# The first units and the first weights of a fused attention and two-MLP kernel in another order

## The chip, the cores and the metric

The kernel runs on one core of a Trainium2 chip. The metric is the time of one execution on the device in microseconds. Three runs of the kernel before took 1079.28, 1087.26 and 1090.63 us; their median, 1087.26 us, is the time before. The engines are TensorE (PE in the rows; PEld is its weight load), VectorE (DVE), ScalarE (ACT), GpSimd (POOL) and SyncE (SP). ACTq and SPq are the instruction queues of ScalarE and SyncE, which also issue DMAs.

## The reference

Decay attention over q, k, v of shape (4, 8, 576, 64), then two MLPs on 2304 tokens of 512 features. In short:

```
log_f  = log(clip(f, 0.0001, 1.0));  cum = cumsum(log_f, axis=-1)
scores = q @ k.T / sqrt(64) + cum[..., :, None] - cum[..., None, :]   # causal
attn   = softmax(scores);  x = attn @ v          # x: (2304, 512)
h = x @ w1_in;  x = (h * sigmoid(1.702 * h)) @ w1_out    # 512 -> 2048 -> 512
h = x @ w2_in;  out = (max(h,0) + alpha * min(h,0)) @ w2_out
```

The MLP weights come as float64 and everything is computed to nearly float32 precision: an operand is split into a rounded high part and a low part (KH, KL and so on), and a product is the sum of three.

## The kernel before

**The plan.** The kernel does not issue its work directly. Each piece is added to a list with a cost per engine that could do it, the buffers it reads and writes, and a priority (`Plan.add`). `Plan.run` then simulates the list: at each step it takes, among all pieces whose inputs are there, the one that can start first, and only between equal start times the one with the lower priority number. A DMA on SP or on ScalarE (`ACTQ`) holds its queue for 480 ns in this plan and ends 1150 ns plus transfer plus 750 ns later. A piece that several engines may do goes to the one that would end it first, with a bias. The order found is the order of the program on each engine; on the chip every engine follows it strictly, so an instruction that waits holds all those behind it. Buffers of a pool (SBUF tiles, PSUM banks) are handed out in the order in which the code created them.

**The start.** f is loaded (L365), clipped (L421) and its logarithm taken (L422). Then the running sums of log f are made in two parts, positions 0 to 255 and 256 to 575 (L427 on): transposes on TensorE (`lf_tr`, L434), copies (`lf_cp`, L439), products with a triangle (`cum_mm`, L448), evacuation by ScalarE (L457), rounding and subtraction on VectorE (L458, L459), and two DMAs to a DRAM scratch (L462, L463). Both parts have priorities near -80, ahead of all units.

**Units.** Attention is cut into 32 units: first positions 0 to 255 of all 16 pairs of heads, then the rest. `prep` loads k and q of a unit in four DMAs each (L510, tiles rk and rq), transposes them (L514), splits them, and loads the sums into DK: the first four units straight from SBUF (L530), the others from the scratch (L535). It loads v (L544, tile VR). The k and q loads of the first 16 units may go to SP or to ScalarE. `chunk` makes the scores once (L598), masks them and finds row maxima (L607, tile MX), and turns these into DQ (L623, L632, L634). `chunk2` makes the scores again with the maxima taken off (L659), the exponential (L663), the product with v (L679) and the division (L718 to L738); the result goes to xr. k and q have two raw buffers each and one buffer for the transposed form.

**The first MLP.** Its first 8 of 16 slices of weights (wA) are loaded and converted from float64 while the first units run (`weight`, `convert`: a DMA at L471 into one of three raw buffers, then L475 to L483 and a split, on ScalarE, VectorE and GpSimd, through two work buffers wc). When the four units of a batch are done, `mlp1a` runs their 256 tokens through these 8 slices: L751 and L793 are its products, L757 and L758 the activation. The tokens and partial sums go to DRAM; the other 8 slices and the second MLP follow on blocks of 512 tokens (L875, L904).

Priorities: unit i is prepared at 100 + i - 2 and computed at 100 + i, slice m of the weights at 105 + 0.6 m, `mlp1a` at 1000 and more.

Of the kernel before, what the change touches and what calls it, by code (L numbers as in the profile page):

```python
# [7 lines left out]
F32 = mybir.dt.float32  # L8
F32R = mybir.dt.float32r
I32 = mybir.dt.int32  # L10
U32 = mybir.dt.uint32
AF = mybir.ActivationFunctionType
# [58 lines left out]
class Plan:  # L71
# [32 lines left out]
    def run(self):  # L104
        free = {}
        dma = 0.0
        avail = [o for o in self.ops if o.nd == 0]
        out = []
        while avail:
            best = None  # L110
            for o in avail:
                t0 = o.ready
                need = {}
                for b in o.bufs:
                    t0 = max(t0, b.begin)
                    if b.pool is not None and b.slot is None:
                        p = b.pool
                        r = p.ready()
                        i = need[p] = need.get(p, -1) + 1
                        if p.nxt + i != b.idx or len(p.free) <= i or p.nxt + i - p.gone >= p.n or r is None:  # L120
                            t0 = None
                            break
                        t0 = max(t0, r, p.free[i][0])
                if t0 is None:
                    continue
                alt = None
                for eng, dur, *more in o.alts:
                    bias, port = (*more, 0.0, False)[:2] if len(more) < 2 else more
                    t = max(t0, free.get(QUEUE.get(eng, eng), 0.0))
                    if port:  # L130
                        t = max(t, free.get("port", 0.0))
                    if eng in QUEUE:
                        end = max(t + 1150.0, dma) + dur + 750.0
                    else:
                        end = t + dur
                    key = end + bias
                    if alt is None or key < alt[0]:
                        alt = (key, t, eng, end, port)
                _, t, eng, end, port = alt
                if best is None or (t, o.pri, end, o.seq) < best[0]:  # L140
                    best = ((t, o.pri, end, o.seq), o, eng, port)
# [4 lines left out]
            if eng in QUEUE:  # L146
                free[QUEUE[eng]] = t + 480.0
                dma = end - 750.0
# [9 lines left out]
            for b in o.bufs:  # L158
                b.left -= 1
                b.end = max(b.end, end + LAT)  # L160
                if b.left == 0 and b.pool is not None:
                    p = b.pool
# [19 lines left out]
def kernel(  # L182
# [13 lines left out]
    nc = tc.nc  # L196
# [4 lines left out]
    P = 128  # L201
    BH = B * H
    NP = H // 2
    KT = DM // P
# [4 lines left out]
    EARLY = 4  # L209
    ACTQ = 16  # L210
    PRE = 2
# [3 lines left out]
    BLK = 256  # L215
    SPLIT = 256

    plan = Plan()
    E = {"PE": nc.tensor, "DVE": nc.vector, "ACT": nc.scalar, "POOL": nc.gpsimd, "SP": nc.sync, "ACTQ": nc.scalar}


    const = ctx.enter_context(tc.tile_pool(name="const", bufs=1))
# [20 lines left out]
    def sb(reg, nm, slots, shape, dt=F32, after=()):  # L243
        p = Pool(slots, after)

        def make(i):
            side, cl = closing[reg]
            return open_region(reg, side, cl).tile(shape, dt, name=f"{nm}{i}", tag=f"{nm}{i}")

        p.make = make  # L250
        return p
# [5 lines left out]

    wA = sb("res", "wA", NA, [P, 2, 2 * KT, P], F32R)
    p_raw8 = sb("res", "wraw", 3, [P, 4, P, 2], I32)
    p_wc = sb("res", "wc", 2, [P, 4, P])  # L260
    p_xh = sb("m1a", "xh", 3, [P, 2, BLK], F32R)
    p_xl = sb("m1a", "xl", 2, [P, 2, BLK], F32R)
    p_g = {n: sb("m1a", n, 2, [P, BLK], d) for n, d in (("gg", F32), ("gh", F32R), ("gl", F32R))}
# [60 lines left out]
    ident = const.tile([P, P], F32, name="ident")  # L324
    ident_r = const.tile([P, P], F32R, name="ident_r")
    alpha_sb = const.tile([P, NM], F32, name="alpha_sb")
    order = tc.manual_schedule()
    order.__enter__()

# [35 lines left out]
    plan.add(DMA(BH * S * 4), lambda e: nc.sync.dma_start(f_sb(), f.rearrange("b h s -> (b h) s")), (), [b_f], -100)  # L365

    def set_ident(e):
        nc.gpsimd.memset(ident, 0.0)
        nc.gpsimd.affine_select(ident, ident, pattern=[[-1, P]], compare_op=ALU.not_equal, fill=1.0, base=0, channel_multiplier=1)

# [50 lines left out]
    plan.add([("DVE", 370.0)], lambda e: nc.vector.tensor_scalar(f_sb(), f_sb(), 1e-4, 1.0, op0=ALU.max, op1=ALU.min), (), [b_f], -80)  # L421
    plan.add([("ACT", 600.0)], lambda e: nc.scalar.activation(f_sb(), f_sb(), AF.Ln), (), [b_f], -80)  # L422

    b_ch = Buf()
    chi = lambda: xr[0:BH, 3, RING - S:].bitcast(F32R)
    b_lt = Buf(ps_h)
    for part, (lo, hi) in enumerate(((0, SPLIT), (SPLIT, S))):  # L427
        ts_ = [t for t in range(NKT) if lo <= t * P < hi]
        pri = -80 + part

        def lf_tr(e, ts_=ts_):
            for t in ts_:
# [30 lines left out]
        plan.add(DMA(128 * (hi - lo)), lambda e, cs=cs: nc.sync.dma_start(cscr[1, :, cs], cuml()[:, cs].bitcast(F32)), [(b_cc, part)], [(b_cum, (part, 1))], pri + 0.5)  # L463
    plan.add(DMA(8192), lambda e: nc.sync.dma_start(alpha_sb, alpha.rearrange("(m p) -> p m", p=P)), (), [b_alpha], 300)

    def convert(wb, half, src, pri):

        raw, w = Buf(p_raw8), Buf(p_wc)
        sl = slice(half * KT, (half + 1) * KT)
        n = KT * P  # L470
        plan.add(DMA(P * n * 8), lambda e: nc.sync.dma_start(raw.ap.rearrange("p c n t -> p c (n t)"), src), (), [raw], pri)  # L471
        low, high = lambda: raw.ap[:, :, :, 0], lambda: raw.ap[:, :, :, 1]
        wi = lambda: w.ap.bitcast(I32)

# [9 lines left out]
        plan.add(a_copy(n), lambda e: copy(e, wb.ap[:, 0, sl], w.ap), [w], [(wb, (half, 0))], pri)  # L484
        plan.add(a_sub(n), lambda e: sub(e, wb.ap[:, 1, sl], w.ap, wb.ap[:, 0, sl].bitcast(F32)), [w, (wb, (half, 0))], [(wb, (half, 1))], pri)

    def weight(pool, w_in, w_out, m, pri):
        wb = Buf(pool)
        convert(wb, 0, w_in[:, m * P:(m + 1) * P].bitcast(I32).rearrange("(c p) n -> p c n", p=P), pri)
        convert(wb, 1, w_out[m * P:(m + 1) * P, :].bitcast(I32).rearrange("p (c n) -> p c n", c=KT), pri + 0.1)  # L490
        return wb

    W1, W2 = {}, {}
# [318 lines left out]

    b_xs, b_yp, b_y1 = Buf(), Buf(), Buf()
    done = {"c": 0}
    A0, A1 = 100.0, 10.0

    def advance(t, pri):
        while done["c"] < NT // BLK and (done["c"] + 1) * BLK <= t:
# [4 lines left out]
    seq = [(b, hp, q0, q1) for q0, q1 in ((0, SPLIT), (SPLIT, S)) for b in range(B) for hp in range(NP)]  # L823
    pend = []
    for i, (b, hp, q0, q1) in enumerate(seq):
        unit = prep(b, hp, q0, q1, A0 + i - PRE, i < EARLY, i < ACTQ)
        pend.append((chunk(unit, q0, q1, A0 + i), col0(b, q0) + q1 - q0 if hp == NP - 1 else 0))
        if i == NP:
            for m in range(NA):
                W1[m] = weight(wA, w1_in, w1_out, m, A0 + 5 + m * 0.6)  # L830
        if len(pend) > 1:
            x, t = pend.pop(0)
            chunk2(x)
            advance(t, 0)
# [124 lines left out]
```

## Time and profile before

| | |
|---|---|
| median of three runs | 1087.26 us (1079.28 to 1090.63) |
| profiled execution | 1090.33 us, span 1088.6 us |
| TensorE busy | 1040.8 us (96% of the span), 6531 matmuls |
| VectorE busy | 696.0 us (64%) |
| ScalarE busy | 448.3 us (41%) |
| GpSimd busy | 124.8 us (11%) |
| mean granted TensorE clock | 0.98 of full speed |

The span goes from the first to the last instruction; the profiled execution's own time is 1.7 us longer than it. The page's row of forty slices of the span (27 us each) shows TensorE at 4, 8, 6 and 7 tenths in the first four and at 9 or more until the last, and its granted clock below full speed in the first five. Matmuls overlap each other and their ends are modelled, so a busy TensorE is not one at its peak.

### The profile page before, as it was taken

What the parts mean: (1) busy time and instruction counts of PE and PEld (TensorE: products, weight loads), DVE (VectorE), ACT (ScalarE), POOL (GpSimd) and SP (SyncE); (2) the same over time, 40 slices, a digit from 0 to 9 for tenths busy, and PEclk for the clock granted to TensorE, in tenths of its full rate; (3) what the DMA queues carried; (4) which work ended last, traced back from release to release, by engine and by line L of the source; (5) the groups of instructions that cost most, each with busy time, mean ns of one, the idle gap of its engine ahead of it and who ended that gap; (6) DMA issues with size and microseconds to landing.
All of it is one profiled execution on the core that took longest, in us unless ns stands there. A gap on an engine that the chain in (4) does not pass through costs nothing.

```text
span 1088.6 us, 17737 instructions
## 1 busy us (share of the span) xinstructions
PE 1040.8 (96%) x6531; PEld 885.5 (81%) x6531; DVE 696.0 (64%) x1560; ACT 448.3 (41%) x1041; POOL 124.8 (11%) x196
## 2 busy tenths in 40 slices
PE   4867999999999999999999999999999999999997
PEld 2656888898999988998888888788888888888885
DVE  5878887788879875969963459743534333544433
ACT  3656655665555554857742347310201211211101
POOL 5321221221221211000100001200000000000000
PEclk8887899999999999999999999999999999999999
DMA  4666564242332110755742325400100200100001
GB/s 76 136 170 156 126 152 97 44 94 47 63 74 60 42 33 10 246 153 176 230 135 97 107 87 177 134 1 1 68 1 1 67 1 1 39 21 20 1 1 39
DMA packets 170055, 86.54 MB, mean 79 GB/s; under 512 B 127440, under 2 KB 155280, under 8 KB 169968
## 3 DMA queue, kind: packets, MB, share of 16 engines
q1 hardware_dynamic: 159360, 84.13, 28.7%
q10 hardware_dynamic: 10608, 1.28, 0.8%
q8 instruction: 51, 0.84, 0.3%
q14 instruction: 36, 0.29, 0.1%
HBM read 66.34 MB, written 19.02 MB: 78 GB/s over the span
## 4 chain that ended last, share of the span: by engine, by line
PE 69%; DVE 4%; ACT 1%; issue 1%; DMA 1%; SPq 0%; ACTq 0%
PE bk L751 30%; PE bk L904 18%; PE bk L875 8%; PE bk L793 5%; PE bk L659 3%; PE bk L708 2%; PE bk L598 1%; PE bk L685 1%; DVE wraw L480 0%; DVE wB L357 0%; PE bk L679 0%; DMA wraw<-in_moe_w_in_dram 0%; DVE wc L483 0%; DVE qgg L762 0%; DVE qgl L357 0%
## 5 line engine op out<-in xcount | busy, mean ns | idle before, releaser
L352 ACT CAST qgh<-qgg 128x512 fp32r<-128x512 f32 (+1 forms) x120 | 69.2, 577 | 337.6 <-DVE qgg L765 314.7
L762 DVE TENSOR_SCALAR qgg<-bk,alpha_sb 128x512 f32<-128x512 f32 (+1 forms) x80 | 55.5, 695 | 166.8 <-PE bk L751 166.8
L751 PE MATMUL bk<-qx,wB 128*128 128x512 f32 (+1 forms) x720 | 156.9, 370 | 0.0
L751 PEld LDWEIGHTS bk<-qx,wB 128*128 128x128 f32 x720 | 125.9, 188 | 24.5
L751 PE MATMUL bk<-xh,wA 128*128 128x256 f32 x576 | 122.6, 293 | 2.6 <-DVE wA L357 1.5
L357 DVE TENSOR_TENSOR qgl<-qgg,qgh 128x512 fp32r<-128x512 f32 (+1 forms) x116 | 75.4, 650 | 67.6 <-ACT qgh L352 59.0
L751 PE MATMUL bk<-qx,wA 128*128 128x512 f32 (+1 forms) x480 | 104.2, 369 | 0.0
L751 PEld LDWEIGHTS bk<-xh,wA 128*128 128x128 f32 x576 | 95.7, 192 | 10.4 <-issue 3.8
L751 PEld LDWEIGHTS bk<-qx,wA 128*128 128x128 f32 x480 | 83.9, 188 | 16.4
L793 PE MATMUL bk<-gh,wA 128*128 128x256 f32 x576 | 85.3, 292 | 6.4 <-ACT DQ L632 2.4
L607 DVE CUSTOM_DVE_ANT_0 bk<-bk,mask 128x512 f32<-128x512 f32 (+3 forms) x160 | 75.0, 493 | 15.5 <-PE bk L598 12.0
L793 PEld LDWEIGHTS bk<-gh,wA 128*128 128x128 f32 x576 | 76.2, 196 | 9.6 <-ACT DQ L632 2.5
L751 PE MATMUL bk<-xl,wA 128*128 128x256 f32 x288 | 81.9, 284 | 1.1 <-DVE xl L357 1.1
L663 ACT ACTIVATE e<-bk 128x320 f32<-128x320 f32 (+3 forms) x224 | 65.2, 365 | 29.9 <-PE bk L659 28.2
L904 PE MATMUL bk<-wA,qgh 128*128 128x512 f32 x288 | 74.1, 396 | 0.5 <-ACT qgh L352 0.5
L904 PEld LDWEIGHTS bk<-wA,qgh 128*128 128x128 f32 x288 | 53.6, 188 | 14.0 <-ACT qgh L352 1.2
L357 POOL TENSOR_TENSOR qx<-qxb,qx 128x512 fp32r<-128x512 f32 (+1 forms) x12 | 15.0, 1257 | 432.9 <-ACT qx L352 387.7
L751 PEld LDWEIGHTS bk<-xl,wA 128*128 128x128 f32 x288 | 55.4, 192 | 1.3 <-DVE xl L357 1.3
L667 POOL TENSOR_SCALAR_AFFINE_SELECT e<-e 128x256 f32<-128x256 f32 (+1 forms) x80 | 32.7, 421 | 199.4 <-ACT e L663 175.8
L475 ACT ACTIVATE wc<-wraw 128x512 f32<-128x512 f32 x64 | 43.2, 678 | 28.8 <-DVE wA L357 9.4
L904 PE MATMUL bk<-wB,qgh 128*128 128x512 f32 x216 | 54.4, 391 | 0.0
L875 PE MATMUL bk<-qgh,wB 128*128 128x512 f32 (+1 forms) x240 | 54.3, 368 | 0.0
(149 smaller groups left out, 2052.9 us busy)
## 6 DMA issues: line engine op xcount, KB each, us to landing
wraw<-in_moe_w_in_dram SPq DMA_DIRECT2D x32, 512.0 KB
wraw<-in_moe_w_out_dram SPq DMA_DIRECT2D x32, 512.0 KB
xscr<-xr SPq DMA_DIRECT2D x9, 512.0 KB
rk<-in_k_dram SPq DMA_DIRECT2D x64, 72.0 KB
ypscr<-yp SPq DMA_DIRECT2D x18, 256.0 KB
VR<-in_v_dram SPq DMA_DIRECT2D x32, 128.0 KB
qxb<-xscr SPq DMA_DIRECT2D x16, 256.0 KB
qyp<-ypscr SPq DMA_DIRECT2D x16, 256.0 KB
```

Source lines behind the costliest of these rows:

```text
L352: nc.scalar.copy(dst, src)
L357: E[e].tensor_tensor(dst, a, b, op=ALU.subtract)
L475: plan.add([("ACT", c_act(n))], lambda e: nc.scalar.mul(w.ap, high().bitcast(F32), 2.0 ** -112), [raw], [w], pri)
L607: plan.add([("DVE", c_dve(c1 - c0) + 90.0)], lambda e, pm=pm, c0=c0, c1=c1, mk=mk, m0=m0, col=col: nc.vector.tensor_tensor_reduce(pm.ap[:, ...
L659: nc.tensor.matmul(pss[hh].ap[:w, :m], x.ap[r, a:a + w], y.ap[r, s0 - q0:n], start=i == 0, stop=i == 3)
L663: plan.add([("ACT", c_act(m, True))], lambda e, hh=hh, pss=pss, e32=e32, w=w, m=m: nc.scalar.activation(e32.ap[:w, hh, :m], pss[hh].ap[:w, ...
L667: plan.add([("POOL", 150.0 + 0.82 * 2 * w, 0.0, True)], lambda e, e32=e32, w=w: nc.gpsimd.affine_select(e32.ap[:w, :, :w], e32.ap[:w, :, : ...
L751: nc.tensor.matmul(ph.ap[:, :n], wb.ap[:, a, c, :], x(c), start=(c == 0 and i == 0), stop=(c == KT - 1 and i == 2))
L762: plan.add([("DVE", c_dve(n) + 56)], lambda e: nc.vector.tensor_scalar(g.ap[:, :n], ph.ap[:, :n], 0.0, alpha_sb[:, m:m + 1], op0=ALU.min, ...
L793: nc.tensor.matmul(py[d // 2].ap[:, d % 2 * BLK:(d % 2 + 1) * BLK], W1[m].ap[:, a, KT + d, :], g.ap, start=(m == 0 and i == 0 and a == 0 a ...
L875: nc.tensor.matmul(py[d].ap[:, :n], W1[m].ap[:, a, KT + d, :], g.ap[:, :n], start=(m == NA and i_ == 0 and a == 0), stop=(m == NM - 1 and ...
L904: nc.tensor.matmul(py[t].ap, g.ap[:, t * P:(t + 1) * P], wo[:, a, KT * P:], start=(m == 0 and i_ == 0 and a == 0), stop=(m == NM - 1 and i ...
```

## The change

The assumed latency of a DMA in the plan rises from 1150 to 1500 ns. The first two units' k and q loads may go to SP only. A one-element exponential (`warm`) is put behind the logarithm. The second part of the sums gets priority 104.5 in place of -79. The first 8 slices of weights get 104 + 0.6 m in place of 105 + 0.6 m, and the loads of the slices 0 and 1 get 101 and 102. There is a third work buffer wc.

```diff
@@ -130,7 +130,7 @@
                     if eng in QUEUE:
-                        end = max(t + 1150.0, dma) + dur + 750.0
+                        end = max(t + 1500.0, dma) + dur + 750.0
@@ -215,6 +215,7 @@
+    A0 = 100.0
@@ -257,7 +258,7 @@
-    p_wc = sb("res", "wc", 2, [P, 4, P])
+    p_wc = sb("res", "wc", 3, [P, 4, P])
@@ -324,6 +325,7 @@
+    warm = const.tile([1, 1], F32, name="warm")
@@ -365,6 +367,7 @@
     def set_ident(e):
+        nc.gpsimd.memset(warm, 0.0)
@@ -421,12 +424,13 @@
+    plan.add([("ACT", 1300.0)], lambda e: nc.scalar.activation(warm, warm, AF.Exp), [b_f, b_id], (), -79)
...
-        pri = -80 + part
+        pri = -80 if part == 0 else A0 + 4.5
@@ -463,12 +467,12 @@
-    def convert(wb, half, src, pri):
+    def convert(wb, half, src, pri, lpri=None):
...
-        plan.add(DMA(P * n * 8), lambda e: nc.sync.dma_start(raw.ap.rearrange("p c n t -> p c (n t)"), src), (), [raw], pri)
+        plan.add(DMA(P * n * 8), lambda e: nc.sync.dma_start(raw.ap.rearrange("p c n t -> p c (n t)"), src), (), [raw], pri if lpri is None else lpri)
@@ -484,10 +488,10 @@
-    def weight(pool, w_in, w_out, m, pri):
+    def weight(pool, w_in, w_out, m, pri, lpri=None):
@@ -823,11 +826,11 @@
-        unit = prep(b, hp, q0, q1, A0 + i - PRE, i < EARLY, i < ACTQ)
+        unit = prep(b, hp, q0, q1, A0 + i - PRE, i < EARLY, 2 <= i < ACTQ)
...
-                W1[m] = weight(wA, w1_in, w1_out, m, A0 + 5 + m * 0.6)
+                W1[m] = weight(wA, w1_in, w1_out, m, A0 + 4 + m * 0.6, A0 + 1 + m if m < 2 else None)
```

## Rows read from the trace of the kernel before

**Rows 1.** Stages: length, each engine's busy us (instructions), granted clock, DMA share, GB/s.

```profile
0.00:20.00 20.00, 6.01 (x27) 3.03 (x27) 9.23 (x30) 6.14 (x11) 13.32 (x40) 1.00 0.43 77
20.00:30.50 10.50, 8.16 (x50) 6.43 (x52) 6.06 (x24) 3.10 (x8) 2.18 (x4) 0.52 0.57 113
64.00:72.00 8.00, 5.18 (x28) 4.62 (x30) 6.21 (x18) 5.63 (x15) 1.09 (x2) 0.57 0.60 151
81.00:92.00 11.00, 8.57 (x52) 6.66 (x50) 6.95 (x18) 7.15 (x18) 0.81 (x2) 0.54 0.46 123
0.00:128.00 128.00, 91.29 (x681) 72.39 (x681) 96.39 (x307) 70.63 (x177) 39.44 (x79) 0.84 0.57 135
128.00:1088.60 960.60, 949.50 (x5852) 813.12 (x5851) 599.59 (x1254) 377.70 (x866) 85.41 (x117) 1.00 0.26 72
```

**Rows 2.** Same view (order PE, PEld, DVE, ACT, POOL), 27 to 108 us.

```profile
27.00:108.00 81.00, 61.18 (x482) 49.35 (x481) 66.41 (x212) 47.57 (x122) 19.53 (x29) 0.84 0.62 154
```

**Rows 3.** ScalarE in time order: start, duration, instruction, [idle before, releaser].

```profile
0.81 0.91 ACTq L510 DMA_DIRECT2D rk<-in_k_dram  x2
1.76 1.28 ACT L352 ACT_TABLE_LOAD   x1 [1.76 <-PEq L943]
3.05 0.30 ACT L352 CAST ident_r<-ident 128x128 fp32r<-128x128 f32 x1
5.29 1.97 ACTq L510 DMA_DIRECT2D rq<-in_q_dram  x2
7.29 1.28 ACT L422 ACT_TABLE_LOAD   x1 [3.94 <-DMA rq<-in_q_dram]
8.59 0.68 ACT L422 ACTIVATE xr<-xr 32x576 f32<-32x576 f32 x1
```

**Rows 4.** VectorE in time order, from the clip to the first mask.

```profile
2.97 0.92 DVE L421 TENSOR_SCALAR xr<-xr 32x576 f32<-32x576 f32 x1 [2.97 <-DMA xr<-in_f_dram]
...
16.24 0.32 DVE L458 CAST xr<-xr 32x320 fp32r<-32x320 f32 x1 [0.95 <-ACT xr L457]
...
16.99 0.48 DVE L459 TENSOR_TENSOR xr<-xr 32x320 fp32r<-32x320 f32 x1
...
17.87 0.27 DVE L607 CUSTOM_DVE_ANT_0 bk<-bk,mask 128x128 f32<-128x128 f32 x1
```

**Rows 5.** TensorE in time order, 0 to 17 us.

```profile
9.41 0.65 PE L434 MATMUL bk<-ident,xr 32*128 32x32 f32 x5 [9.41 <-ACT xr L422]
10.44 4.49 PE L448 MATMUL bk<-xr 128*32 128x256 f32 x14 [0.38 <-DVE xr L439]
...
16.43 0.33 PE L598 MATMUL bk<-DK,ones 64*128 64x128 f32 x2 [1.25 <-DMA DK<-xr]
```

**Rows 6.** SP's DMA issues in time order, first 15 us.

```profile
0.81 0.40 SPq L365 DMA_DIRECT2D xr<-in_f_dram  x1
...
4.21 1.45 SPq L510 DMA_DIRECT2D rk<-in_k_dram  x3
...
13.14 0.32 SPq L462 DMA_DIRECT2D cscr<-xr  x1
...
14.03 1.25 SPq L530 DMA_DIRECT2D DK<-xr  x2
```

**Rows 7.** ScalarE in time order, around the first exponential.

```profile
23.90 1.28 ACT L663 ACT_TABLE_LOAD   x1 [1.80 <-DMA rq<-in_q_dram]
25.20 0.38 ACT L663 ACTIVATE e<-bk 128x256 f32<-128x256 f32 x1
```

**Rows 8.** SP, ScalarE and TensorE in time order, lines that concern early weights.

```profile
27.06 0.45 SPq L471 DMA_DIRECT2D wraw<-in_moe_w_in_dram  x1
...
61.77 0.66 ACT L475 ACTIVATE wc<-wraw 128x512 f32<-128x512 f32 x1 [2.04 <-DMA wraw<-in_moe_w_in_dram]
...
66.82 0.91 PE L659 MATMUL bk<-DQ,DK 64*128 64x256 f32 x2 [3.77 <-ACT DQ L632]
```

**Rows 9.** Waits of TensorE, 0 to 128 us: us in total, times, longest.

```profile
PE bk L751 <- DVE wA L357: 1.5, 2, 1.1
```

More of the change, by code (lines that the diff above doesn't have):

```diff
@@ L485, in convert @@
         plan.add(a_sub(n), lambda e: sub(e, wb.ap[:, 1, sl], w.ap, wb.ap[:, 0, sl].bitcast(F32)), [w, (wb, (half, 0))], [(wb, (half, 1))], pri)
-    def weight(pool, w_in, w_out, m, pri):
+    def weight(pool, w_in, w_out, m, pri, lpri=None):
         wb = Buf(pool)
-        convert(wb, 0, w_in[:, m * P:(m + 1) * P].bitcast(I32).rearrange("(c p) n -> p c n", p=P), pri)
-        convert(wb, 1, w_out[m * P:(m + 1) * P, :].bitcast(I32).rearrange("p (c n) -> p c n", c=KT), pri + 0.1)
+        convert(wb, 0, w_in[:, m * P:(m + 1) * P].bitcast(I32).rearrange("(c p) n -> p c n", p=P), pri, lpri)
+        convert(wb, 1, w_out[m * P:(m + 1) * P, :].bitcast(I32).rearrange("p (c n) -> p c n", c=KT), pri + 0.1, lpri)
         return wb
@@ L814 @@
     done = {"c": 0}
-    A0, A1 = 100.0, 10.0
     def advance(t, pri):
```

## The prediction

> **What bounds the kernel now.** I read the stage table first, then the time order of single engines at the start. TensorE bounds the run. After 128 us it is busy 949.5 of 960.6 us at the full clock; before 128 us only 91.3 of 128, at a mean granted clock of 0.84 [rows 1]. So what a new order can give lies in the first 128 us: 36.7 us of idle time, and about 91.3 x 0.16 = 14.6 us lost because part of the work runs at 1.2 GHz. Single stretches show that second loss: 20 to 30.5, 64 to 72 and 81 to 92 us have granted clocks of 0.52 to 0.57, each after a gap on TensorE [rows 1]. From 27 to 108 us VectorE is busy 66.4 of 81 us: nearly a bound of its own, as all conversions and masks go through it [rows 2]. I assume that work moved earlier on TensorE in this first part shortens the end one for one, since nothing after 128 us waits.
>
> The order at the start is set by ScalarE. It loads a table until 3.04 us and casts until 3.35, then issues two loads of q from 5.29 to 7.26, and only then loads the table for the logarithm, which runs from 8.59 to 9.27 [rows 3]. The input of that logarithm was ready at 2.97 + 0.92 = 3.89 us [rows 4]. TensorE waits for it from the start, 9.41 us [rows 5]; SP stands until 13.14 us for the first half of the sums [rows 6]; the first product with DK comes at 16.43 us [rows 5].
>
> **The change part by part.** The profiled execution took 1090.33 us (span 1088.6); the median of the three runs is 3.07 us lower, 1087.26. The sum is made against 1090.33 and carried over to the median.
>
> *Loads of units 0 and 1 leave ScalarE.* Without the two q issues the logarithm's table load can follow the cast: 3.35 + 1.28 = 4.63, after the 3.89 of its input, so the logarithm starts near 4.65 instead of 8.59, 3.9 us earlier. The chain behind it (transposes, products, evacuation, rounding, DMA into DK) took 16.43 - 9.27 = 7.2 us, so the first product with DK moves to 12.5. Cover needed: units 0 and 1 then have 16 loads of q and k and 4 of v on SP, 20 in all. Three of SP's take 1.45 us, 0.48 each [rows 6]; after f, at 1.21 us, that is 20 x 0.48 = 9.6 us, ending at 10.8, and DK's two issues (1.25 us) can go by 12.1 if all 20 stand ahead of them. The sums reach SP 3.9 us earlier than 13.14, at 9.2; with the planner's priorities the write of the sums goes ahead of the last loads. So SP hides it, with little room. Price: -3.9; bounds 0 (SP is late by as much) and -5.
>
> *Units 2 to 15 may still be put on ScalarE.* Unit 2's loads become free once the first transposes are done, near 5 us, and SP then has a backlog, so they go to ScalarE, in front of the evacuation of the sums (L457). Bounds: 0, and +2.0 (a pair of issues lasted 1.97) [rows 3]. I take +0.9, the other pair of that row group (0.91), since the long one is not explained by anything the trace shows.
>
> *Early table for the exponential.* The load of 1.28 us at 23.90 stands right in front of the first exponential at 25.20 [rows 7], whose result unit 0 waits for. It moves behind the logarithm (4.65 + 0.68 = 5.3 to 6.6 us), plus one activation of one element and one memset of one element on POOL, which I cost at nothing: ScalarE's next work there, the cast of unit 0's k, took place at 9.18 before, and its q comes later still. Cover gone: 1.28 us on the first cast. Price -1.3; bounds 0 (the scores are late for another reason) and -1.3. The Trainium skill (ScalarE: Activation LUTs, What ACT_TABLE_LOAD costs) puts a switch at about 2.66 us, the load and a drain; the exponential 0.02 us after the load's end shows no drain here, and by the page the sum would be 1.4 us lower. The same page (Table sets: the hidden batching unit) says that logarithm and exponential share a set, by which nothing would be saved; the row with a load of its own for the exponential speaks against it in this kernel.
>
> *Late half of the sums.* Its rounding and subtraction on VectorE (0.32 and 0.48 us) stand ahead of unit 0's first mask at 17.87 [rows 4], though its inputs were there earlier: -0.8 on the path. They, three small copies and TensorE's products (about 3.0 of the 4.49 us of that row [rows 5]) have to run somewhere. The planner takes the operation that can start first and uses the priority only between equals, and the bank pool hands out buffers in order of creation, so unit 0's output bank can't be taken before the late half's bank has been. So the half moves only some microseconds, into gaps of TensorE. Bounds -0.8 and +3.0 (its products in front of unit 0's scores, not preempted). I take -0.8: gaps of over 3 us are there. Its two DMAs to DRAM are read only by the units from 16 on.
>
> *Weights.* The first weight load is issued at 27.06 us [rows 8]; the conversions get a priority one unit earlier, the loads of m = 0 and 1 four and three units earlier, and there is a third work buffer. Conversion time is the same in sum. TensorE waited 1.5 us in total for the halves that VectorE writes (L751) [rows 9]. Price -1.5; bounds 0 and -6.5 (the second rival below). One unit's preparation is pushed back by as much VectorE work as is pulled forward; it is ahead of TensorE by then.
>
> *Assumed latency 1500 for 1150.* It changes the order of DMAs everywhere, costs no instruction, and after 128 us TensorE has its work ready: 0; bounds -2 and +2 (a fifth of the 11.1 us of idle time there [rows 1]).
>
> Sum: -3.9 + 0.9 - 1.3 - 0.8 - 1.5 = -6.6, so 1083.7 for an execution like the profiled one, and 1080.7 from the median.
>
> **The rivals.** *More than the sum.* At 61.77 us ScalarE stands 2.04 us for a weight transfer, with the row maxima of a unit queued behind it, and TensorE stands 3.77 us until 66.82 and then runs at the low clock [rows 8]. If early weights remove that wait, the stretch 64 to 72 gives back its idle 2.8 us and 5.18 x 0.43 = 2.2 us of clock, 5.0 in all; the stretch 81 to 92 is worth 2.4 + 8.57 x 0.46 = 6.4 in the same way. One or both besides the sum: 1069 to 1076. For it: the cause is a weight that came late. Against: only two of eight are pulled forward, and the load at 61.77 is of a later one.
>
> *Given back.* VectorE's 82% from 27 to 108 us [rows 2] is the limit, and units that start earlier wait for it later; or the transfers set the pace, not the engine that issues them. The latter is the view of the Trainium skill (DMA: Bandwidth & Descriptors, Issuing engines are not separate DMA queues): issuing from several engines saves only issue time, usually little beside the transfer. Against that as a mechanism here: ScalarE's 3.9 us wait ends with its own issue, not with a landing [rows 3]. A quarter to a half of the sum stays: 1084 to 1086.
>
> *Slower, by SP.* If a load on SP costs what the long pair did on ScalarE (0.98 each), 20 loads end at 1.21 + 19.7 = 20.9 us and DK's issue comes 6.9 us later than its 14.03 [rows 6]. Against this stand -1.3 and -0.8: +4.8, and 1092; if the longer gap costs another low stretch, 1097. It decides from (14.03 - 1.21) / 20 = 0.64 us per load, where SP has shown 0.48, and only if the planner leaves all loads in front.
>
> *It doesn't do what it says.* Priorities being ties only, the late half stays ahead of the first masks and the weights come no sooner: -4.3, 1083.
>
> **How the numbers follow.** Forecast 1081 (1077 to 1084): 0.42. More: 0.25. Given back: 0.21. Slower: 0.07. No effect of the priorities: 0.05. The three runs of before lie 11 us apart, so 1% (10.9 us) is about what a measurement can tell. Faster by over 1% is under 1076.4: nearly all of the second case and the lower edge of the first, 0.33. Slower by over 1% (over 1098): the far end of the SP case and the noise, 0.04. The rest 0.63. The range 1068 to 1091 leaves out the rest of the SP case and the lowest of the second.
>
> **What would show it.** The logarithm before 5.5 us, the first product with DK near 12.5 to 13.5, no table load after 10 us, the first exponential about 5 us earlier than 25.20, TensorE's idle time to 128 us near 31 instead of 36.7 us. The prediction is wrong if SP issues DK after 14 us, if the products of the late half stand right in front of unit 0's scores, or if the low-clock stretches after 60 us number more or fewer than before: each weighs as much as the whole forecast.

## The result, and the profile after

The changed kernel takes 1077.09 us (median of 8 runs, 1075.21 to 1078.60) where the kernel before took 1086.49 us beside it (8 runs, 1079.28 to 1090.63): ratio 0.991, 95% interval 0.9891 to 0.993, or 9.4 us less. The forecast was 1081 us from 1087.26, a gain of 6.6; so the time lies in the range, 4 us under the forecast. The profiled execution took 1075.87 us with a span of 1074.1, and is 14.5 us shorter in span than the profiled one of before, which at 1090.33 us was one of the slowest of its kernel. Lines after the new ones are shifted by 2 to 4: L457 is now L461, L598 is L602, L607 is L611, L663 is L667, L751 is L755, L875 is L878 and L904 is L907.

The stages first, with the columns of [rows 1] (length, then busy us of TensorE, weight load, VectorE, ScalarE, GpSimd, granted clock, DMA share, GB/s):

```profile
0.00:20.00 20.00, 9.23 (x48) 5.80 (x49) 9.98 (x35) 8.19 (x16) 13.48 (x41) 0.81 0.51 99
20.00:30.50 10.50, 10.19 (x64) 7.20 (x64) 8.73 (x34) 7.64 (x19) 4.55 (x7) 0.50 0.67 154
64.00:72.00 8.00, 7.39 (x46) 6.18 (x47) 7.55 (x22) 4.89 (x13) 1.92 (x3) 0.61 0.53 144
81.00:92.00 11.00, 10.04 (x88) 8.54 (x88) 10.82 (x32) 8.98 (x25) 4.99 (x6) 1.00 0.60 154
0.00:128.00 128.00, 99.85 (x781) 79.97 (x782) 102.48 (x327) 77.83 (x196) 45.34 (x86) 0.85 0.61 142
128.00:1074.00 946.00, 933.92 (x5752) 806.33 (x5751) 587.84 (x1238) 370.04 (x847) 80.13 (x106) 1.00 0.26 72
```

TensorE is idle for 128 - 99.85 = 28.1 us before 128 us, 36.7 before, and has issued 781 products there instead of 681. Behind that it still has 12 us of idle time.

ScalarE's start answers to [rows 3] and [rows 7] (start, duration, instruction, [idle before, releaser]):

```profile
3.71 0.68 ACT L425 ACTIVATE xr<-xr 32x576 f32<-32x576 f32 x1
4.41 1.28 ACT L427 ACT_TABLE_LOAD   x1
5.70 0.20 ACT L427 ACTIVATE warm<-warm 1x1 f32<-1x1 f32 x1
...
10.32 1.91 ACTq L514 DMA_DIRECT2D rq<-in_q_dram  x4
12.35 1.85 ACTq L514 DMA_DIRECT2D rk<-in_k_dram  x2
14.24 0.43 ACT L461 ACTIVATE xr<-bk 32x320 f32<-32x320 f32 x1 [5.79 <-DMA rq<-in_q_dram]
...
19.98 0.83 ACT L667 ACTIVATE e<-bk 128x256 f32<-128x256 f32 x3
```

The logarithm starts at 3.71 instead of 8.59 us, the first exponential at 19.98 instead of 25.20, with no table load in front of it. But ScalarE is idle for 5.79 us before the late half's evacuation (14.24). Up to 10.17 us the products that it reads are still running (the row at 5.57 below, 4.60 us long); for the other 4 us it stands behind six loads, issued from 10.32 to 14.20, that the planner put on ScalarE for later units. VectorE passes that on; the same view of VectorE, for [rows 4]:

```profile
14.71 0.51 DVE L462 CAST xr<-xr 32x320 fp32r<-32x320 f32 x1 [3.04 <-ACT xr L461]
15.14 0.40 DVE L359 TENSOR_TENSOR KL<-tk,KH 128x256 fp32r<-128x256 f32 x1
15.47 0.28 DVE L611 CUSTOM_DVE_ANT_0 bk<-bk,mask 128x128 f32<-128x128 f32 x1
```

The first mask starts at 15.47, though its scores were done at 13.0: it is behind the late half's rounding on its engine. TensorE and SP for [rows 5], [rows 6] and [rows 8]:

```profile
5.57 4.60 PE L452 MATMUL bk<-xr 128*32 128x256 f32 x14 [0.38 <-DVE xr L443]
...
12.11 0.35 PE L602 MATMUL bk<-DK,ones 64*128 64x128 f32 x2 [1.69 <-DMA DK<-xr]
12.24 0.53 PE L602 MATMUL bk<-KH,QH 64*128 64x256 f32 x2
12.51 0.48 PE L602 MATMUL bk<-DK,ones 64*128 64x256 f32 x2
17.17 0.42 PE L627 MATMUL bk<-ident_r,MX 128*99 128x128 f32 x1 [4.17 <-DVE MX L611]
...
64.61 0.96 PE L663 MATMUL bk<-DQ,DK 64*128 64x256 f32 x2 [6.40 <-DVE DQ L638]
```

```profile
9.22 0.67 SPq L534 DMA_DIRECT2D DK<-xr  x1
...
14.51 0.40 SPq L475 DMA_DIRECT2D wraw<-in_moe_w_in_dram  x1
```

All 14 products of the sums still run in one block (4.60 us), so the late half was not deferred on TensorE. The first weight load is issued at 14.51 instead of 27.06. The stall of 3.77 us near 66 us [rows 8] did not go: it is 6.40 us now, and ends with VectorE's part of DQ instead of ScalarE's.

**Where the 14.5 us between the spans are.** In every kernel of this study the same 3,771 products stand ahead of the first one of line L875 (L878 after), so that product, between 480 and 490 us, is a clean milestone:

```profile
486.70 1.98 PE L875 MATMUL bk<-qgh,wB 128*128 128x512 f32 x8
```

```profile
480.32 1.98 PE L878 MATMUL bk<-qgh,wB 128*128 128x512 f32 x8
```

(Before first, then after.) 6.4 us are gained up to there, though single profiles of one order differ by as much as 4.4 us in it (E1 below). The rest, 1088.6 - 486.7 = 601.9 us, has become 1074.1 - 480.3 = 593.8 us: 8.1 us come from a stretch that no edit of the order aims at, and in which TensorE hardly waits. There the profile shows this, in time order from the kernel before and then from the changed one:

```profile
726.79 4.36 PE L751 MATMUL bk<-qx,wB 128*128 128x512 f32 x18
730.99 1.98 PE L904 MATMUL bk<-wB,qgh 128*128 128x512 f32 x8
...
999.66 0.63 PE L904 MATMUL bk<-wA,qgh 128*128 128x512 f32 x2
1000.13 1.10 PE L904 MATMUL bk<-wA,qgl 128*128 128x512 f32 x4
1001.07 2.03 PE L904 MATMUL bk<-wA,qgh 128*128 128x512 f32 x8
1002.93 1.10 PE L904 MATMUL bk<-wA,qgl 128*128 128x512 f32 x4
```

```profile
723.46 4.24 PE L755 MATMUL bk<-qx,wB 128*128 128x512 f32 x18
727.54 1.98 PE L907 MATMUL bk<-wB,qgh 128*128 128x512 f32 x8
...
999.76 1.98 PE L907 MATMUL bk<-wA,qgh 128*128 128x512 f32 x8
1001.58 1.07 PE L907 MATMUL bk<-wA,qgl 128*128 128x512 f32 x4
```

The same eighteen products start over 730.99 - 726.79 = 4.20 us before and over 727.54 - 723.46 = 4.08 us after: 233 and 227 ns each, at the full clock, with no wait. Eight products of wA and qgh go from 1002.93 - 1001.07 = 1.86 to 1001.58 - 999.76 = 1.82 us. The engine's busy time can't show it, as it is 100% in both.

What differs is the placement. The 4-byte tile `warm` takes 32 bytes on the left side of SBUF, and every left-hand tile behind it (wA, wC, wraw, the second qx) moves by 32 bytes modulo 64; the right-hand ones (wB, the first qx, qgh, qgl) stay. In the addresses that the built programs give their tiles, the first wA starts at byte 33984 before (0 modulo 64) and the first qgh at 219104 (32 modulo 64); after, that wA is at 34016, 32 modulo 64 as well. Products whose stationary and moving operand differ by 32 modulo 64 run at the slower pace.

### The profile page after: what moved, and what is told of

Read it like the earlier page. It is cut to its first block, busy times and chain, and to the rows that moved or that the text cites. A ratio compares the mean times of both kernels' runs of the same rounds, so it can differ in the third digit from the quotient of the medians.

```text
span 1074.1 us, 17787 instructions
## 1 busy us (share of the span) xinstructions
PE 1033.8 (96%) x6531; PEld 886.3 (83%) x6531; DVE 690.3 (64%) x1565; ACT 447.9 (42%) x1042; POOL 125.5 (12%) x192
## 4 chain that ended last, share of the span: by engine, by line
PE 51%; DVE 3%; DMA 2%; ACT 1%; issue 0%; SPq 0%; DVEq 0%; ACTq 0%
PE bk L755 26%; PE bk L907 18%; PE bk L878 6%; DMA wraw<-in_moe_w_out_dram 1%; PE bk L797 1%; DVE wraw L484 1%; DVE wA L359 1%; DVE wc L487 0%; DVE qgg L762 0%; ACT wraw L480 0%; DVE qgl L359 0%; ACT wc L479 0%; DMA qxb<-xscr 0%; DVE wc L481 0%; DMA out_dram<-qyp 0%
## 5 line engine op out<-in xcount | busy, mean ns | idle before, releaser
L755 PE MATMUL bk<-qx,wB 128*128 128x512 f32 (+1 forms) x720 | 155.8, 368 | 0.0
L755 PEld LDWEIGHTS bk<-qx,wB 128*128 128x128 f32 x720 | 125.9, 189 | 22.7
L755 PE MATMUL bk<-xh,wA 128*128 128x256 f32 x576 | 120.6, 292 | 0.0
L755 PE MATMUL bk<-qx,wA 128*128 128x512 f32 (+1 forms) x480 | 103.6, 368 | 0.0
L755 PEld LDWEIGHTS bk<-xh,wA 128*128 128x128 f32 x576 | 95.3, 192 | 7.0 <-issue 4.0
L755 PEld LDWEIGHTS bk<-qx,wA 128*128 128x128 f32 x480 | 84.2, 188 | 15.3
L797 PE MATMUL bk<-gh,wA 128*128 128x256 f32 x576 | 82.9, 287 | 3.9 <-ACT gh L354 3.2
L755 PE MATMUL bk<-xl,wA 128*128 128x256 f32 x288 | 81.9, 284 | 1.1 <-DVE xl L359 1.1
L611 DVE CUSTOM_DVE_ANT_0 bk<-bk,mask 128x512 f32<-128x512 f32 (+3 forms) x160 | 75.2, 492 | 10.1 <-PE bk L602 8.3
L797 PEld LDWEIGHTS bk<-gh,wA 128*128 128x128 f32 x576 | 73.8, 191 | 7.6 <-ACT gh L354 3.9
L667 ACT ACTIVATE e<-bk 128x320 f32<-128x320 f32 (+3 forms) x224 | 66.5, 364 | 22.4 <-PE bk L663 21.4
L907 PE MATMUL bk<-wA,qgh 128*128 128x512 f32 x288 | 71.9, 389 | 0.0
L907 PEld LDWEIGHTS bk<-wA,qgh 128*128 128x128 f32 x288 | 53.8, 188 | 11.0
L671 POOL TENSOR_SCALAR_AFFINE_SELECT e<-e 128x256 f32<-128x256 f32 (+1 forms) x80 | 33.6, 432 | 208.4 <-ACT e L667 180.6
L755 PEld LDWEIGHTS bk<-xl,wA 128*128 128x128 f32 x288 | 55.4, 192 | 1.4 <-DVE xl L359 1.3
L878 PE MATMUL bk<-qgh,wB 128*128 128x512 f32 (+1 forms) x240 | 54.3, 368 | 0.8 <-ACT qgh L354 0.8
L907 PE MATMUL bk<-wB,qgh 128*128 128x512 f32 x216 | 53.9, 390 | 0.0
L755 PE MATMUL bk<-qx,wC 128*128 128x512 f32 (+1 forms) x240 | 52.8, 368 | 0.0
```

What stands on the lines that cost most here:

```text
L611: plan.add([("DVE", c_dve(c1 - c0) + 90.0)], lambda e, pm=pm, c0=c0, c1=c1, mk=mk, m0=m0, col=col: nc.vector.tensor_tensor_reduce(pm.ap[:, ...
L667: plan.add([("ACT", c_act(m, True))], lambda e, hh=hh, pss=pss, e32=e32, w=w, m=m: nc.scalar.activation(e32.ap[:w, hh, :m], pss[hh].ap[:w, ...
L671: plan.add([("POOL", 150.0 + 0.82 * 2 * w, 0.0, True)], lambda e, e32=e32, w=w: nc.gpsimd.affine_select(e32.ap[:w, :, :w], e32.ap[:w, :, : ...
L755: nc.tensor.matmul(ph.ap[:, :n], wb.ap[:, a, c, :], x(c), start=(c == 0 and i == 0), stop=(c == KT - 1 and i == 2))
L797: nc.tensor.matmul(py[d // 2].ap[:, d % 2 * BLK:(d % 2 + 1) * BLK], W1[m].ap[:, a, KT + d, :], g.ap, start=(m == 0 and i == 0 and a == 0 a ...
L878: nc.tensor.matmul(py[d].ap[:, :n], W1[m].ap[:, a, KT + d, :], g.ap[:, :n], start=(m == NA and i_ == 0 and a == 0), stop=(m == NM - 1 and ...
```

## The experiments

Placement and order were separated first. All ratios are to the kernel before, run beside the experiment on the same chip; where an experiment is set against the changed kernel or against another one, the difference is that of the two ratios, times 1087 us. (A ratio is worked out from all runs and need not be the quotient of the two medians given; the two differ by up to 1.5 us.) The changed kernel itself was not run again beside the experiments.

**E1, placement alone.** The kernel before, with a tile that nothing uses:

```diff
+    warm = const.tile([1, 1], F32, name="warm")
```

> The kernel before, with only the declaration of the one-element tile (4 bytes, taking 32) and no instruction on it: the order of all work stays, the tiles on the left side of SBUF (weights wA and wC, one of the two x tiles) move by 32 bytes. Theory PLACEMENT (of the 14.5 us between the two profiled spans about 8.4 are the pace of the 512-column matmuls after 480 us, which start 231 to 235 ns apart where the two operands' addresses differ by 32 modulo 64 bytes, and 227 where they agree; the new tile shifted the left side): 6 to 9 us faster than before, 1078 to 1081, 512-column matmuls 227 ns apart throughout, the first 128 us as before. Theory START (all of the gain comes from the order of the first 128 us, and the pace differs from execution to execution by itself): 1085 to 1088, no change.

Measured: 1079.91 us against 1086.90, ratio 0.9924 (0.9903 to 0.9946). So 7.0 us, of the changed kernel's 9.4, come without one instruction more or in another place. PLACEMENT is right and START falls. In its profile the rest behind the milestone takes 1077.9 - 482.3 = 595.6 us. The milestone itself is at 482.35 us, 4.4 us sooner than in the profile of before with the same order of work: in single profiles it can differ by that much without any change of the order.

**E2, order alone.** The changed kernel with the first tile 64 bytes long, so that the left side stands modulo 64 as before:

```diff
-    warm = const.tile([1, 1], F32, name="warm")
+    warm = const.tile([1, 16], F32, name="warm")[:, 0:1]
```

> The changed kernel with the same tile 64 bytes wide, so that the left side stands as in the kernel before modulo 64; order of all work as in the changed kernel. PLACEMENT: 6 to 9 us slower than the changed kernel, 1083 to 1086, with 231 to 235 ns again where a tile of the left meets one of the right. START: 1077, unchanged against the changed kernel.

Measured: 1081.72 against 1086.90, ratio 0.9947 (0.9927 to 0.9968), 4 us over the changed kernel by the ratios, where 6 to 9 were expected. The rest behind the milestone takes 1083.8 - 482.3 = 601.5 us, as in the kernel before.

**E9, both sides shifted.** The changed kernel, with 32 bytes at the top of the right side too:

```diff
+    ctx.enter_context(tc.tile_pool(name="pad", bufs=1, side="right")).tile([1, 1], F32, name="pad")
     open_region("att", "right")
```

> The changed kernel with a second tile of 4 bytes at the top of the right side of SBUF, which moves every right-hand tile (wB, qx0, qgh) by 32 bytes as the first one moved the left-hand tiles; no instruction is added and the plan stays the same. Theory DIFFERENCE (a 512-column product is slow where its stationary and its moving operand differ by 32 bytes in their addresses modulo 64): the two sides differ again, so the slow pace of the kernel before comes back, some 8 us of it after 480 us: 1081 to 1084 us, like the run in which the changed kernel's first tile took 64 bytes (1081.7). Rival ABSOLUTE (what matters is where the left side alone stands): pace and time stay those of the changed kernel, 1075 to 1079 us.

Measured: 1086.0 against 1086.88, ratio 0.9993 (0.9973 to 1.0013); 601.0 us behind the milestone. DIFFERENCE is right and ABSOLUTE falls: the left side stands as in the fast kernel, and the pace is the slow one. The time came out 2 us above what DIFFERENCE expected, and 5.0 us above E2 by the ratios, although E2 has the same plan and the same pace, with the mean granted clock at 0.978 (12 runs) against 0.980 (6 runs). They ran on different chips; why they differ stays open. Twenty microseconds in the second half, columns as above, of before, E1, the changed kernel and E9 in turn:

```profile
720.00:740.00 20.00, 20.00 (x88) 16.18 (x87) 6.96 (x11) 1.86 (x3) 0.00 (x0) 1.00 0.00 1
```

```profile
720.00:740.00 20.00, 20.00 (x90) 16.57 (x89) 8.36 (x12) 2.48 (x4) 0.00 (x0) 1.00 0.00 0
```

```profile
720.00:740.00 20.00, 20.00 (x89) 16.54 (x89) 7.44 (x11) 1.86 (x3) 0.00 (x0) 1.00 0.00 0
```

```profile
720.00:740.00 20.00, 20.00 (x88) 16.22 (x87) 6.90 (x11) 1.86 (x3) 0.00 (x0) 1.00 0.00 1
```

The count of products in a window of full busy time is what to read: 88 or 90 products, at busy time 20.00 and clock 1.00 each time (in some windows of the changed kernel 89, as a window's edges cut). Mean distance of the starts of 512-column products, by pair, worked out from all of them after 480 us:

| pair (sides) | before | E1 | after | E9 |
|---|---|---|---|---|
| wA, qgh (left, right) | 233.2 ns | 227.4 | 227.1 | 233.3 |
| qx, wB (both, right) | 230.3 | 226.8 | 226.7 | 230.3 |
| wB, qgh (right, right) | 229.2 | 227.2 | 227.2 | 229.4 |

The pair that differs in every product is slow in nearly all of them (at least 94% start more than 229 ns apart); qx, wB differs for one of the two qx only. Split by qx, its products start 233.4 ns apart with the qx of the left side and 227.2 with that of the right in the kernel before, 233.4 and 227.1 in E9, where the right-hand pair stands at 0 modulo 64 instead of 32. Over all pairs of the kernel before, the 1,109 products that differ start 233.2 ns apart on average and the 1,284 that agree 227.9; in E1 and the changed kernel none differs, and the means are 227.0 and 226.9. Summed over the products after 480 us, what lies above 226.7 ns is 8.8 us before, 8.5 in E2 and E9, 0.4 to 0.7 in E1, the changed kernel and all other experiments.

**The parts of the order.** The other eight keep the placement of the changed kernel.

E3 gives the first two units' loads back to ScalarE:

```diff
-        unit = prep(b, hp, q0, q1, A0 + i - PRE, i < EARLY, 2 <= i < ACTQ)
+        unit = prep(b, hp, q0, q1, A0 + i - PRE, i < EARLY, i < ACTQ)
```

> The changed kernel with the loads of units 0 and 1 allowed on ScalarE again. If these loads hold the logarithm (the prediction's first term, 3.9 us): logarithm after 7 us, first product with DK 3 to 4 us later than 12.1, and 2 to 4 us slower than the changed kernel, 1079 to 1081. Rival: the planner, now with the longer latency, puts few of them there, or the later stretch takes the loss up: within 1.5 us of 1077.

Measured: 1078.91, ratio 0.9914 (0.9893 to 0.9935), 0.4 us over the changed kernel. The logarithm is back at 7.89 us and the first product with DK at 15.54 instead of 12.11; almost none of these 3.4 us is in the time, near what the rival expected. Most of them are gone by the first exponential, 20.80 us against 19.98.

E4 takes the weights back (the work buffer stays):

```diff
-                W1[m] = weight(wA, w1_in, w1_out, m, A0 + 4 + m * 0.6, A0 + 1 + m if m < 2 else None)
+                W1[m] = weight(wA, w1_in, w1_out, m, A0 + 5 + m * 0.6)
```

> The changed kernel with the priorities of the first eight weight slices and of their loads as before. If early weights are worth the predicted 1.5 us: 1078 to 1080. Rival 1, they are worth more (a whole stretch at the low clock): 1082 or more. Rival 2, they cost (the changed trace has a 6.4 us wait of TensorE near 60 us, behind a weight transfer): 1070 to 1075.

Measured: 1083.6, ratio 0.9968 (0.9951 to 0.9985), 6.3 us over the changed kernel: not the predicted 1.5, but the band of rival 1.

E10 does the reverse: E1 with the weights' part of the change and the third buffer, and nothing else of the order.

```diff
-    p_wc = sb("res", "wc", 2, [P, 4, P])
+    p_wc = sb("res", "wc", 3, [P, 4, P])
...
-                W1[m] = weight(wA, w1_in, w1_out, m, A0 + 5 + m * 0.6)
+                W1[m] = weight(wA, w1_in, w1_out, m, A0 + 4 + m * 0.6, A0 + 1 + m if m < 2 else None)
```

> The kernel before with the placement of the changed one (the 4-byte tile alone) and, of the change in order, the weights' part only: conversions one unit earlier, two early pairs of loads, a third work buffer. Against 1079.9 us of the kernel before with the placement alone. Theory WEIGHTS (the earlier weights carry the gain in order, as taking them back cost 6.5 us): 1073 to 1077 us, the wait of 2 to 4 us on TensorE for a transposed input near 66 us shorter. Rival TOGETHER (no part carries it; each edit reshuffles the whole plan, and the sum is not made of parts): 1079 to 1085 us. By the prediction's term of -1.5 it would be 1078.4 us.

Measured: 1082.33, ratio 0.9961 (0.9939 to 0.9982), 4.0 us over E1 (the intervals touch). WEIGHTS falls: the part that costs 6.3 us when it is taken out gains nothing when it is put in alone, as TOGETHER expected.

E12 puts the weights one unit earlier again:

```diff
-                W1[m] = weight(wA, w1_in, w1_out, m, A0 + 4 + m * 0.6, A0 + 1 + m if m < 2 else None)
+                W1[m] = weight(wA, w1_in, w1_out, m, A0 + 3 + m * 0.6, A0 + m if m < 2 else None)
```

> The changed kernel with conversions and early loads of the weights one unit earlier again (A0 + 3 and A0 + m). Theory WEIGHTS (the sooner the MLP can be fed, the sooner TensorE is full): 1072 to 1076 us, first MLP product before 54.2 us. Rival VECTORE (conversions then push back the preparation of units 4 and 5 on VectorE, which is busy over 80% there): 1078 to 1084 us, a new idle stretch on TensorE before 54 us.

Measured: 1078.82, ratio 0.9924 (0.9896 to 0.9953): not told apart from the changed kernel. WEIGHTS falls: the first product of L797 came at 64.3 us, against 54.2 in the changed kernel, and the first of L755 at 37.3 against 36.7, so the earlier priority brought neither earlier. The sign of VECTORE is there without a loss that the intervals show: from 30 to 54 us TensorE is idle 9.2 us instead of 4.5, and its longest wait there is for the row maxima that VectorE makes:

```profile
51.93 0.42 PE L627 MATMUL bk<-ident_r,MX 128*99 128x128 f32 x1 [2.86 <-DVE MX L611]
```

E5 gives the late half its old priority:

```diff
-        pri = -80 if part == 0 else A0 + 4.5
+        pri = -80 + part
```

> The changed kernel with the late half of the sums at its old priority. The prediction costs its deferral at -0.8 us; in the changed trace TensorE runs both halves in one block all the same, and the late half's evacuation waits behind loads on ScalarE and holds the first mask. Theory TIES (priorities decide only between equals, so the edit moves little): within 1.5 us of the changed kernel. Rival: with the old priority the evacuation goes ahead of the loads, the first mask comes up to 3 us earlier and the kernel is 1.5 to 3 us faster, 1074 to 1076.

Measured: 1082.84, ratio 0.9957 (0.9941 to 0.9972), 5.1 us over the changed kernel. Both expectations missed. The evacuation came 2.0 us sooner (12.26) and the first mask 1.3 us (14.13), but the first exponential did not (20.18 us), and the milestone came at 486.9.

E6 leaves out the one-element exponential:

```diff
-    plan.add([("ACT", 1300.0)], lambda e: nc.scalar.activation(warm, warm, AF.Exp), [b_f, b_id], (), -79)
```

> The changed kernel without the one-element exponential (its tile and memset stay, so all addresses stay). Prediction: the table load of 1.28 us is back in front of the first exponential, 1.0 to 1.5 us slower, 1078 to 1078.6. Rival: the first exponential is late for other reasons (its scores) and the load hides behind them: no change.

Measured: 1076.9, ratio 0.9898 (0.9875 to 0.992): no loss, at most a gain of 1.3 us that the intervals don't show. The table load is back in front of the exponential:

```profile
19.23 1.28 ACT L666 ACT_TABLE_LOAD   x1
20.53 0.38 ACT L666 ACTIVATE e<-bk 128x256 f32<-128x256 f32 x1
```

20.53 against 19.98 us: of the 1.28 us of the load 0.73 were hidden.

E7 takes ScalarE's loads away up to unit 4:

```diff
-        unit = prep(b, hp, q0, q1, A0 + i - PRE, i < EARLY, 2 <= i < ACTQ)
+        unit = prep(b, hp, q0, q1, A0 + i - PRE, i < EARLY, 4 <= i < ACTQ)
```

> The changed kernel with units 2 and 3 kept off ScalarE too. In the changed trace ScalarE waits 5.8 us with the evacuation of the late half behind loads of units 2 and 3, VectorE stands 3.0 us behind it and the first mask starts at 15.5 us though its scores ended at 13. If that block is the cause: evacuation before 11 us, first mask near 13, 1.5 to 3 us faster. Rival: SP then carries 40 loads in a row, DK of the first units goes later, and the time is the same or up to 3 us longer.

Measured: 1085.59, ratio 0.9977 (0.9961 to 0.9992), 7.3 us over the changed kernel, more than either expectation allowed. The wait for the late half went as it should. ScalarE, then VectorE:

```profile
11.13 0.43 ACT L461 ACTIVATE xr<-bk 32x320 f32<-32x320 f32 x1 [3.39 <-PE bk L452]
...
17.07 1.19 ACT L667 ACTIVATE e<-bk 128x256 f32<-128x256 f32 x4 [1.74 <-PE bk L663]
```

```profile
12.50 0.28 DVE L611 CUSTOM_DVE_ANT_0 bk<-bk,mask 128x128 f32<-128x128 f32 x1
```

Mask and exponential come 3.0 and 2.9 us sooner, TensorE is idle 24.4 us instead of 28.1 before 128 us, and the run is slower. Two stretches show why, first of the changed kernel, then of E7:

```profile
72.00:100.00 28.00, 23.52 (x206) 19.57 (x206) 27.50 (x81) 23.74 (x60) 9.97 (x14) 1.00 0.72 184
100.00:128.00 28.00, 26.53 (x245) 22.04 (x242) 25.03 (x81) 17.76 (x50) 6.54 (x10) 1.00 0.56 133
```

```profile
72.00:100.00 28.00, 23.18 (x154) 19.26 (x154) 24.19 (x62) 18.07 (x44) 4.72 (x7) 0.76 0.58 155
100.00:128.00 28.00, 25.46 (x217) 21.90 (x211) 23.99 (x74) 18.58 (x49) 7.07 (x11) 0.94 0.62 154
```

Nearly the same busy time holds 451 products in the one and 371 in the other: in E7 TensorE falls to 1.2 GHz again after 72 us, in the changed kernel it does not until 128 us. Up to 128 us E7 has 54.1 - 28.5 = 25.6 us more of its busy time at 1.2 GHz; half of that is lost, 12.8 us, less 3.7 us of idle time saved: 9.1 us, where the milestone comes 8.4 us later.

E8 leaves the loads and plans the late half's evacuation later:

```diff
-        plan.add([("PE", 1350.0 if part == 0 else 3300.0)], cum_mm, [(b_cl, i) for i in range(part + 1)] + [b_tri], [bb], pri)
+        plan.add([("PE", 1350.0 if part == 0 else 3300.0)], cum_mm, [(b_cl, i) for i in range(part + 1)] + [b_tri], [bb], pri, lag=0.0 if part == 0 else 9000.0)
```

> The changed kernel in which the plan makes the evacuation of the late half ready 9 us later than it is, so that it stands behind the first masks on ScalarE and VectorE. If the late half's place is what holds the first mask: first mask near 13 us, 1.5 to 3 us faster than the changed kernel. Rival: the bank it holds and its later DMAs cost as much: no change.

Measured: 1083.94, ratio 0.9952 (0.9932 to 0.9972), 4.6 us over the changed kernel, though the evacuation went to 24.77 us and the first mask came 0.8 us sooner, at 14.71. Neither expectation held.

E11 puts the assumed latency back:

```diff
-                        end = max(t + 1500.0, dma) + dur + 750.0
+                        end = max(t + 1150.0, dma) + dur + 750.0
```

> The changed kernel with the planner's assumed DMA latency back at 1150. Prediction: no term for it, 1077 us within 2. Theory RESHUFFLE (every edit of the plan at the head moves stalls and low-clock stretches by several us either way): 1079 to 1085 us, with TensorE's idle time plus half its low-clock time before 128 us above 42.4 us in the same measure. If it comes out near 1077 with that sum unchanged, RESHUFFLE is too broad.

Measured: 1084.51, ratio 0.9977 (0.9959 to 0.9995), 7.3 us over the changed kernel, with TensorE's idle time plus half its low-clock time at 30.0 + 33.0 / 2 = 46.5 us. RESHUFFLE fits. A constant that adds no instruction is worth as much as any part of the change.

**All together**, one profile each (low clock: TensorE's busy time at 1.2 GHz before 128 us; rest: from the milestone to the end of the span):

| kernel | ratio | milestone us | rest us | idle to 128 | low clock |
|---|---|---|---|---|---|
| before | 1 | 486.7 | 601.9 | 36.7 | 34.3 |
| after | 0.991 | 480.3 | 593.8 | 28.1 | 28.5 |
| E1 placement alone | 0.9924 | 482.3 | 595.6 | 33.6 | 30.1 |
| E2 order alone | 0.9947 | 482.3 | 601.5 | 25.3 | 39.1 |
| E9 both sides | 0.9993 | 482.3 | 601.0 | 29.4 | 27.3 |
| E6 no exponential | 0.9898 | 481.9 | 593.4 | 28.2 | 43.0 |
| E3 ScalarE loads | 0.9914 | 483.9 | 595.1 | 29.8 | 43.3 |
| E12 weights earlier | 0.9924 | 483.8 | 593.2 | 30.7 | 39.1 |
| E8 evacuation | 0.9952 | 488.3 | 593.8 | 24.8 | 38.9 |
| E5 late half | 0.9957 | 486.9 | 594.2 | 33.3 | 24.6 |
| E10 weights alone | 0.9961 | 482.9 | 597.3 | 29.5 | 36.4 |
| E4 weights back | 0.9968 | 489.3 | 594.8 | 30.6 | 47.6 |
| E7 loads to unit 4 | 0.9977 | 488.7 | 593.6 | 24.4 | 54.1 |
| E11 latency | 0.9977 | 486.0 | 595.5 | 30.0 | 33.0 |

The rest is 601.0 to 601.9 us with the sides apart and 593.2 to 597.3 with them alike: about 7 us, whatever the order. Within one placement the milestone makes most of the difference, and neither idle nor low-clock time up to 128 us foretells it alone (E8 has less idle time than the changed kernel and comes 8 us later). No version beats the changed kernel beyond its interval; E6 equals it with one activation less.

## Why the prediction was right, and where it was not

The number was right and its account only in part: most of the measured gain is a term that the sum put at nothing. That -6.6 came near the measured -9.4 was luck: the order was worth less than the sum said, and the placement, which is not in it, made up for that.

- *Costed at nothing: the tile `warm`.* Here the account failed. The sum priced its memset and its activation, and not that allocating it moves other tiles. E1 gives 7.0 us for the placement alone; by the ratios it is worth 8.3 (E1), 4.0 (E2 against the changed kernel) and 9.0 (E9 against it), and the traces show 7 to 8 (the rest behind the milestone, and the pace). With it fell the assumption that what comes after 128 us stays as it was. What the low clock cost up to there was also put a little low, at 14.6 us from the mean clock: 34.3 us of busy time at 1.2 GHz lose half, 17.2 us.
- *The order as a whole, -6.6.* Measured with placement equal: -1.5 us (changed kernel against E1), -5.8 (E2) and -0.8 (E9, the same plan as E2), by the ratios. So some 1 to 6 us; two of the three don't differ from nothing by their intervals. As E2 and E9 share plan and pace and still lie 5.0 us apart, the worth of a single edit is known to some 5 us. The sum was probably too large, and the second rival, that part is given back, fits better for the order. That it is given back in the clock is argued and not shown: the mean granted clock of the whole run is 0.978 after (mean of 8 runs) against 0.982 before (17 runs beside E1) and 0.983 in E1 (6 runs), and 0.004 of 1077 us would be 4 us; but the two profiles have less time at the low clock up to 128 us after the change (28.5 us) than before (34.3).
- *ScalarE loads, -3.9.* The chain moved as worked out: the logarithm at 3.71 (4.65 predicted), the first product with DK at 12.11 (12.5), DK's issue on SP at 9.22 and not late. But E3 puts its worth at 0.4 us. The sign "first exponential about 5 us earlier" came too, and proves little: E3 has it (20.80) with the logarithm at 7.89. That work moved earlier at the head shortens the end one for one was wrong: E7 moved it 3 us further and lost 7.3.
- *Loads of units 2 to 15 in front of L457, +0.9.* Seen, and mis-sized: of the 5.79 us that ScalarE stood before the late half's evacuation about 4 were the loads', and E7, without them, has the evacuation 3.1 and the first mask 3.0 us sooner, above the bound of 2.0. The Trainium skill (DMA: Bandwidth & Descriptors, Issuing engines are not separate DMA queues) calls an engine's issue time usually little beside the transfer; here it is what the evacuation waited for, though E7 shows that the end did not hang on it.
- *Early table, -1.3.* The load did go, but E6 shows no gain: 0.55 us of it were on the path of the first exponential, and none in the time. The Trainium skill (ScalarE: Activation LUTs, What ACT_TABLE_LOAD costs) adds a drain to each switch; here the logarithm starts 0.01 us after its load (2.42 + 1.28 = 3.70), and the next load 0.02 us after the logarithm's end (4.39), so again no drain is seen. That next load, at 4.41, is the exponential's own, so in this program each of the two has its own load, where the Trainium skill (the same page, Table sets: the hidden batching unit) counts one for both.
- *Late half, -0.8.* That priorities only break ties held on TensorE: one block of 14 products, before the first scores, which the prediction had named as a sign against it. On VectorE the late half stayed ahead of the first mask, and the 0.8 was not had. By E5 the changed priority comes out at 5.1 us all the same, about as much as E2 and E9 differ by; if it is real, it comes from the plan it leads to later on, as the first exponential starts no sooner.
- *Weights, -1.5.* Taken out they cost 6.3, put in alone they gain nothing (E10). No size of its own can be given for the term. (Its bound of -6.5 rests on the first rival, not on the second as it says.)
- *Latency, 0 within 2.* Outside its bounds: 7.3 (E11).
- *The rival "more than the sum"* had its time band (1069 to 1076) just missed by the median. Its mechanism half came: the low-clock stretch at 81 to 92 us [rows 1] is gone in the profile (clock 1.00 there), but the stall near 66 us grew. From 60 to 128 us TensorE fell to the low clock three times before (from 65, 82 and 106 us) and once after (60 to 70 us). The prediction had named a changed number of such stretches as a sign of being wrong; with the late half in front of the first scores, two of its three signs came.

Undoing the parts one at a time costs 0.4 + 6.3 + 5.1 - 1.3 + 7.3 = 17.8 us; undoing all of them (E1) costs 1.5. A sum of terms could not have given the order's worth, since every edit makes another plan for the first 480 us. TensorE's idle time plus half its low-clock time, counted up to the milestone, is 48.0 us in the changed kernel and 59.5 in E4, 57.4 in E7, 53.5 in E5, 53.2 in E8 and 51.7 in E11: 11.5, 9.4, 5.5, 5.2 and 3.7 us more, where the milestone comes 9.0, 8.4, 6.6, 8.0 and 5.7 us later. So most of each loss is waiting and low clock (E5 and E8 also fall to the low clock near 433 us); but E6 has 6.0 us more as well and is only 1.6 us later there. Which stall begins each loss was followed only in E7 and stays open for E4, E5, E8 and E11.

Open is also why the pair wB, qgh, alike modulo 64, runs slow for about half of its products in the kernels whose other pairs differ (in the rows before, it is fast at 730.99). The slow ones mostly follow products that differ: in the kernel before, the first six agreeing products behind such a run start 229 to 231 ns apart on average, the eighth to the eleventh 226.6 to 226.8.

## What to carry to other kernels

Before crediting a reordering, compare the pace of a stretch that it doesn't touch: count the products in equal windows of full busy time, and if they differ, compare the tiles' addresses modulo 64 and rerun the old kernel with a dummy tile of the same size. Where a planner lays out a dense first stage, cost the edits together and test them one by one in both directions, since taking one out and putting it in alone need not have the same sign. A first unit that starts earlier is worth nothing by itself if the engine falls back to the low clock later.

## What the runs showed of the hardware

- 128 x 128 x 512 products whose two SBUF operands differ by 32 bytes modulo 64 in their addresses start 231 to 235 ns apart instead of 226 to 227 at the full clock, 3%; some 7 us of this kernel. The difference counts, not the address (E9). Only 32 bytes was tried.
- The spread of one kernel's times goes with its clock: 29 runs of the kernel before on one chip go from 1080.8 us at a mean granted clock of 0.987 to 1091.4 at 0.980, with a correlation of -0.85. In the profiles most of the time at 1.2 GHz lies before 128 us, so part of what looks like noise is probably how much of the head falls into it.
